# Element-wise work moved from VectorE to GpSimd, and fewer weight tiles converted ahead of the first MoE product

## The chip, the cores and the metric

One Trainium2 chip, one of its cores. The metric is device microseconds (us) of one execution; lower is better. The engines are TensorE (PE, matrix products), VectorE (DVE), ScalarE (ACT), GpSimd (POOL) and SyncE (SP, which issues the transfers). Each engine takes its instructions in the order in which the program issues them.

## The reference

Inputs are float32, the sizes 4 batches, 8 heads, 768 positions, head dimension 48. Three stages follow one another:

```python
state = 0                                    # per batch and head, 48 x 48
for t in range(768):                         # a linear attention with decay
    cur = outer(u * k[t], v[t])
    y[t] = r[t] @ (state + cur)
    state = w[t][:, None] * state + outer(k[t], v[t])
x = y as 3072 tokens x 384
x = (silu(x @ w_gate) * (x @ w_val)) @ w_out          # MoE 1, 384 -> 1536 -> 384
h = x @ w_in                                          # MoE 2, 384 -> 2048 -> 384
out = (h - tanh(h)) @ w_out2
```

## The kernel before, in words

**Attention.** The sequence is cut into chunks of 128 positions, and 24 units of work (4 chunk-and-head groups each, `NU = 24`) are walked two at a time. For each unit VectorE forms the running product of the decays with a scan (`scan`, L201), ScalarE its reciprocal by logarithm and exponential (`lnexp`), and VectorE the scaled keys `kt` (`ekx`, `ktq`) and the queries `q = r * P` (L258). TensorE multiplies `kt` by `q` (`sc`, L290), VectorE writes the upper triangle of the result over a tile `A` (`mask`, L296) whose diagonal ScalarE has filled (`fill`, L241) with the sums of r * u * k (`diag`: two products, L226 and L230, and a reduction, L233). The state is carried from chunk to chunk (`tr`, `kv`, `state`, `spread`), and `y` adds both parts (L350, L357). `out` splits y into a high and a low part for the products that follow; the rows of the last heads are put in place by six small transfers (`place`, L390), so that the tokens' tile `x` of a block of 512 tokens is complete only when these have landed.

**Order by hand.** The schedule is manual. `gap(n)` holds the attention's work as steps, nine for two units (113 in all), each a set of chains that `weave` interleaves instruction by instruction, so that the issue order is the program's. The first 25 steps run on their own; then one step goes ahead of each of the MoE's steps. A block of 512 tokens has 18 MoE steps in the first pass (6 hidden tiles, three steps each: a gate product, a value product, an output product of an earlier tile), nine matmuls of 128x128 by 128x512 each. Four units make a block; there are 6 blocks. The second pass over the MoE's other half and MoE 2 come after and have no attention in them.

**Weights.** The weights arrive as 64-bit floating-point numbers in tiles `f` of 128x384 (L71). `converter.step` puts the bits of a float32 together on VectorE (L93, L95, L97), ScalarE casts that to the high part (L77), and VectorE subtracts to get the low part (`low`, L82); cast and low part are issued in the next tile's step. Two tiles beyond the one in conversion have their load issued, with three buffers. The first 18 tiles (`c1`) serve the first blocks; 12 of them are converted ahead of the first MoE product, two before the first attention step and ten in the odd steps from 5 to 23, and then one in every second MoE step. The other tiles (`cb`) follow from the second block on, one in four steps, and go to memory.

All loads and stores are issued by SP, in the program's order, so that one that waits for its buffer or its data holds up those behind it. GpSimd only prepares constants at the start.

Of the kernel before, what the change touches and what calls it, by code (L numbers as in the profile page):

```python
# [8 lines left out]
FP32 = mybir.dt.float32  # L9
# [5 lines left out]
ALU = mybir.AluOpType  # L15
# [14 lines left out]
UB = NU // NB  # L30
# [19 lines left out]
def weave(chains):  # L50

    live = [c for c in chains if c is not None]
    while live:
        live = [c for c in live if next(c, live) is not live]


def once(fn):
    fn()
    yield


class converter:


    def __init__(self, nc, f64, stage):
        self.nc, self.f64, self.stage = nc, f64, stage
        self.loaded, self.sub = [], None

    def load(self, src):
        st = self.f64.tile([128, 384], I64, tag="f64", name="f64")  # L70
# [8 lines left out]
    def low(self):  # L79
        if self.sub:  # L80
            w, wt = self.sub
            self.nc.vector.tensor_tensor(wt[:, 1, :], w, wt[:, 0, :].bitcast(FP32), ALU.subtract)  # L82
            self.sub = None

    def step(self, wt, guard=False):
# [28 lines left out]
class attention:  # L114
# [105 lines left out]
        self.nc.scalar.activation(  # L220
            out=w, in_=w, func=AF.Relu, bias=self.wmx, accum_out=self.accw[:, u:u + 1])

    def diag(self, u):
        nc, s = self.nc, self.u[u]
        r, k = s["rk"][:, 0, :], s["rk"][:, 1, :]
        nc.vector.tensor_tensor(r, r, k, ALU.mult)  # L226
        yield
        r4 = r.rearrange("p (a c e) -> p a c e", a=2, c=2)
        ub = self.u_sb[:, u % 2, :].rearrange("p (a e) -> p a e", a=2)
        nc.vector.tensor_tensor(r4, r4, ub[:, :, None, :].to_broadcast([128, 2, 2, 96]), ALU.mult)  # L230
        yield
        s["c"] = self.odd.tile([128, 8], FP32, tag="c", name="c")
        nc.vector.tensor_reduce(s["c"], r.rearrange("p (c d) -> p c d", d=D), AX.X, ALU.add)  # L233
        yield
# [13 lines left out]
        nc.vector.tensor_tensor(s["x0"], self.k(u), s["x0"], ALU.mult)  # L248
        yield

    def ktq(self, u):
        nc, s = self.nc, self.u[u]
        s["kt"] = self.wk.tile([128, 4, 128], FP32, tag="kt", name="kt", bufs=1)
        nc.vector.scalar_tensor_tensor(
            s["kt"], s["e"], 2.0, s["x0"], ALU.subtract, ALU.mult, reverse0=True)
        yield
        s["q"] = self.wk.tile([128, 4, 128], FP32, tag="q", name="q")
        nc.vector.tensor_tensor(s["q"], self.r(u), s["P"][:, :, 0:128], ALU.mult)  # L258
        yield

    def chunks(self, u):

# [132 lines left out]
    def gap(self, n, xt, xtile):  # L395

        gi, n = divmod(n, 9)
        u0, u1, n0, n1 = range(2 * gi, 2 * gi + 4)  # L400
        up = u0 - 1
        here, ahead, behind = u0 < NU, n0 < NU, gi > 0
        x = lambda u: xt[u // UB]
        c = []
        if n == 0:
            if behind:
                c.append(self.state(up))
            if here:
                self.sc(u0)
                self.load_v(u1)  # L410
            if ahead:
                c.append(self.scan(n0))
        elif n == 1:
            if behind:
                self.spread(up)
            if here:
                c.append(self.mask(u0))
            if ahead:
                c.append(self.scan(n1))
                self.load_rk(n0)  # L420
        elif n == 2:
            if here:
                self.tr(u0)
            if behind:
                self.y(up)
            if here:
                c.append(self.ekx(u1))
            if ahead:
                self.lnexp((n0, n1))
        elif n == 3:  # L430
            if here:
                self.trc(u0)
                c.append(self.ktq(u1))
            if behind:
                c.append(self.out(up, x(up)))
            if here:
                c.append(once(lambda: self.fill(u1)))
            self.load_w(u0 + 4)
            self.load_v(n0)
        elif n == 4:  # L440
            if behind:
                self.place(up, x(up))
            if here:
                self.kv(u0)
                self.sc(u1)
            if ahead:
                c.append(self.diag(n0))
        elif n == 5:
            c += [self.state(u0), self.mask(u1)]
            if ahead:  # L450
                c.append(once(lambda: self.w_check(n0)))
            self.load_rk(n1)
            self.load_tok(u0 + 4)
        elif n == 6:
            self.spread(u0)
            self.tr(u1)
            if ahead:
                c.append(self.diag(n1))
                c.append(once(lambda: self.w_check(n1)))
        elif n == 7:  # L460
            self.trc(u1)
            self.y(u0)
            if ahead:
                c.append(self.ekx(n0))
            self.load_w(u0 + 5)
            self.load_tok(u0 + 5)
        else:
            if u0 % UB == 0:
                xt[u0 // UB] = xtile()
            self.kv(u1)  # L470
            c.append(self.out(u0, x(u0)))
            if ahead:
                c.append(self.ktq(n0))
                c.append(once(lambda: self.fill(n0)))
        return c

# [2 lines left out]
def body(ctx: ExitStack, tc: tile.TileContext, rkw, tok, vtok, ub, w1, w2, rf, kf, vf, wf, uf, out):  # L479
    nc = tc.nc  # L480
# [30 lines left out]
    conv = converter(nc, f64, stage)  # L511
# [149 lines left out]
    with tc.manual_schedule():  # L661

        pa = ExitStack()
        att = attention(nc, pa, tc, const, (rkw, tok, vtok, ub), accw, accx)
        pp_ = pa.enter_context(tc.tile_pool(name="pp", bufs=1))

        c1 = convs(seq(0), w1, wpa, W)
# [20 lines left out]
        nc.vector.memset(zsw_t, -ZSW)  # L688

        xt, ptin = {}, {}  # L690
        weave([att.scan(0)])
        weave([att.scan(1)])
        att.lnexp((0, 1))
        c1.step()
        nc.vector.tensor_copy(out=att.cm, in_=att.cmf)
        weave([att.diag(0), att.ekx(0)])
        weave([att.ktq(0), att.diag(1), c1.chain(), once(lambda: att.fill(0))])
        att.w_check(0)
        att.w_check(1)
        att.load_tok(2)  # L700
# [4 lines left out]
        def agap():  # L705
            if at[0] == steps:
                return []
            at[0] += 1
            return att.gap(at[0] - 1, xt, xtile)

        for n in range(9 * UB // 2 + 7):
            weave(agap() + ([c1.chain()] if n % 2 and n > 4 else []))

        tail = None
        for b in range(NB):
            last = b == NB - 1
            if last:
                cb.until(3 * HF)
                pa.close()
                ex = ctx.enter_context(tc.tile_pool(name="ex", bufs=3, space=PSUM))  # L720
                wpb = ctx.enter_context(tc.tile_pool(name="wpb", bufs=3 * HF))
                pb = ExitStack()
                pin = pb.enter_context(tc.tile_pool(name="pin", bufs=2))
                x2p = pb.enter_context(tc.tile_pool(name="x2p", bufs=1))
                for i in cb.order:
                    fetch(wpb, i, W)

            def gap(f, i, b=b, last=last):
                j = 3 * f + i
                chains = [] if last else agap()  # L730
                if b == 0:
                    if j % 2:
                        chains.append(c1.chain())
                    if c1.n <= j:
                        c1.until(j)
                elif b == 1 and j == 0:
                    c1.until(3 * HF)
                    cb.loads(2)
                elif j % 4 == 2:
                    chains.append(cb.chain())  # L740
                return chains

            def done(a, b=b):
                if b == NB - 1:
                    t = pin.tile([128, KD, TB], FP32, tag="pin", name="pin")
                elif b == NB - 2:
                    t = x2p.tile([128, 2, KD, TB], FP32R, tag="x2", name="x2")[:, 0].bitcast(FP32)
                else:
                    t = pp_.tile([128, KD, TB], FP32, tag="pt", name="pt")

                def copy(k):
                    nc.scalar.copy(out=t[:, k], in_=a[k])
                    if k == KD - 1:
                        if b == NB - 1:
                            ptin[b] = t
                        else:
                            nc.sync.dma_start(out=pt_d[b], in_=t)

                for k in range(KD):
                    later(k // 2, lambda k=k: copy(k))  # L760

            if b + 1 < NB:
                nc.sync.dma_start(out=xs_d[b], in_=xt[b].bitcast(FP32))
            tail = mlp(xt[b], range(HF), tail, gap, done)
# [136 lines left out]
        for j, b in enumerate(order):  # L901
            for m in range(NM):
# [14 lines left out]
                if m == 3 and j + 1 < NB:  # L917
                    n = order[j + 1]
# [26 lines left out]
        with tc.If(flag1 < 384):  # L945
# [3 lines left out]
            with ExitStack() as fb:  # L949
                fw = fb.enter_context(tc.tile_pool(name="fw", bufs=3))  # L950
                with tc.For_i(0, NB, 1) as b:
# [3 lines left out]
                    for f in range(NF):  # L955
                        wt = [fw.tile([128, 2, 384], FP32R, tag=f"fw{i}", name="fw", bufs=1) for i in range(3)]
# [7 lines left out]
                        s, t = stile("s", bufs=1), stile("t")  # L964
# [16 lines left out]
        with tc.If(flag2 < 512):  # L981
# [3 lines left out]
            with tc.For_i(0, NB, 1) as b:  # L985
# [3 lines left out]
                for m in range(NM):  # L989
                    wt = [fw.tile([128, 2, 384], FP32R, tag=f"fw{i}", name="fw") for i in range(2)]  # L990
# [161 lines left out]
```

## Time and profile before

| | |
|---|---|
| median of 3 runs | 1013.29 us (1012.47 to 1013.78) |
| profiled execution | 1014.84 us, span 1013.1 us |
| TensorE, VectorE, ScalarE, GpSimd busy | 958.1, 643.6, 508.6, 3.8 us |
| mean granted clock of TensorE | 0.974 of full speed |

A row of the profile names the engine, the source line (L82 is line 82), the operation and the tiles, output first. Busy times are sums over instructions, means are nanoseconds of one. VectorE's consecutive instructions overlap at their ends, so the distance from start to start is shorter than an instruction's duration. The span is what the profiler sees; the execution's time is some 1.7 us more.

### The profile page before, as it was taken

The page shows a single profiled execution, that of the slowest core. Times are in us where ns is not written, and L with a number is a line of the kernel's source. Part 1 is how long each engine was busy: PE and PEld are TensorE (multiplying, and loading weights), DVE is VectorE, ACT ScalarE, POOL GpSimd, SP SyncE. Part 2 cuts the span into 40 slices and gives each one's busy share as a digit, 9 for nine tenths or more (in the row PEclk, how much of TensorE's full clock was granted, in tenths as well). Part 3 has the DMA queues.
Part 4 walks back from the last instruction along what each step waited for, and adds up shares of the span by engine and source line. Part 5 has one row for each costly group of instructions (what it writes and reads, how often), then busy time and mean ns, then how long its engine had stood idle before and what let it go on. Part 6 is the DMA issues. An engine that isn't in the chain of part 4 may idle for free.

```text
span 1013.1 us, 13589 instructions
## 1 busy us (share of the span) xinstructions
PE 958.1 (95%) x5002; PEld 785.2 (77%) x5002; DVE 643.6 (64%) x1166; ACT 508.6 (50%) x1110; POOL 3.8 (0%) x16
## 2 busy tenths in 40 slices
PE   2679999999999999999999999999999999999994
PEld 2557778888888788888888887888888888888883
DVE  8999878888875424656646635666556665565442
ACT  6668777676764313323323325555455554545541
POOL 1000000000000000000000000000000000000000
PEclk9659999999999999999999999999999999999997
DMA  8567365766643481454557764344353343520001
GB/s 300 168 228 259 113 239 182 257 203 229 217 148 128 159 348 47 164 178 159 200 176 260 259 226 156 94 144 137 97 195 98 111 170 98 197 64 0 32 1 38
DMA packets 53506, 164.09 MB, mean 162 GB/s; under 512 B 6704, under 2 KB 9136, under 8 KB 50608
## 3 DMA queue, kind: packets, MB, share of 16 engines
q1 hardware_dynamic: 53424, 163.06, 47.0%
q8 instruction: 43, 0.70, 0.3%
q14 instruction: 39, 0.32, 0.1%
HBM read 122.14 MB, written 38.54 MB: 159 GB/s over the span
## 4 chain that ended last, share of the span: by engine, by line
PE 85%; DVE 9%; ACT 2%; DMA 1%; issue 1%; SPq 0%; DVEq 0%; ACTq 0%
PE p_ps L523 46%; PE a L872 19%; PE a L651 14%; PE sc_ps L290 2%; PE y_ps L357 2%; DMA f<-in_w_dram 1%; PE y_ps L350 1%; PE kv_ps L307 1%; DVE A L296 1%; DVE cvt L95 1%; DVE P L201 1%; DVE w L82 1%; DVE cvt L97 1%; DVE rk L230 1%; PE kT_ps L270 0%
## 5 line engine op out<-in xcount | busy, mean ns | idle before, releaser
L523 PE MATMUL p_ps<-x,w 128*128 128x512 f32 x2160 | 526.5, 392 | 0.0
L523 PEld LDWEIGHTS p_ps<-x,w 128*128 128x128 f32 x2160 | 402.4, 188 | 88.7 <-issue 3.9
L872 PE MATMUL a<-hi,w 128*128 128x512 f32 x576 | 192.9, 389 | 0.0
L851 DVE TENSOR_TENSOR t<-p_ps,z 128x512 f32<-128x512 f32 x96 | 66.4, 692 | 157.9 <-ACT z L849 157.9
L651 PE MATMUL a<-hi,w 128*128 128x512 f32 x432 | 146.8, 394 | 0.0
L626 DVE TENSOR_TENSOR t<-s,p_ps 128x512 f32<-128x512 f32 x72 | 49.4, 686 | 142.0 <-PE p_ps L523 133.6
L872 PEld LDWEIGHTS a<-hi,w 128*128 128x128 f32 x576 | 108.1, 188 | 22.4
L872 PE MATMUL a<-lo,w 128*128 128x512 f32 x288 | 112.4, 390 | 2.7 <-DVE lo L860 2.7
L849 ACT ACTIVATE z<-p_ps 128x512 f32<-128x512 f32 x96 | 57.5, 599 | 109.6 <-PE p_ps L523 109.5
L854 ACT CAST hi<-g 128x512 fp32r<-128x512 f32 x96 | 59.7, 622 | 77.5 <-DVE g L852 77.5
L617 ACT ACTIVATE s<-p_ps 128x512 f32<-128x512 f32 x72 | 42.9, 596 | 107.8 <-PE p_ps L523 107.7
L651 PEld LDWEIGHTS a<-hi,w 128*128 128x128 f32 x432 | 81.1, 188 | 17.5
L630 ACT CAST hi<-t 128x512 fp32r<-128x512 f32 x72 | 44.7, 621 | 94.8 <-DVE t L626 94.2
L651 PE MATMUL a<-lo,w 128*128 128x512 f32 x216 | 84.3, 390 | 0.0
L852 DVE SCALAR_TENSOR_TENSOR g<-zs,t 128x512 f32<-128x512 f32 x96 | 66.5, 693 | 10.3 <-ACT zs L850 0.5
L850 ACT ACTIVATE zs<-z,sa_t 128x512 f32<-128x512 f32 x96 | 69.7, 726 | 3.1
L872 PEld LDWEIGHTS a<-lo,w 128*128 128x128 f32 x288 | 54.0, 188 | 15.0 <-DVE lo L860 3.9
L860 DVE TENSOR_TENSOR lo<-g,hi 128x512 fp32r<-128x512 f32 x96 | 65.6, 683 | 0.1
L634 DVE TENSOR_TENSOR lo<-t,hi 128x512 fp32r<-128x512 f32 x72 | 49.6, 689 | 19.3 <-ACT hi L630 19.3
L290 PE MATMUL sc_ps<-q,kt 64*128 64x128 f32 x384 | 36.1, 323 | 26.5 <-DVE q L258 25.2
L241 ACT ACTIVATE A<-ident,c 128x128 f32<-128x128 f32 x192 | 58.9, 400 | 2.5 <-DVE c L233 2.5
L290 PEld LDWEIGHTS sc_ps<-q,kt 64*128 64x128 f32 x384 | 30.3, 221 | 31.7 <-DVE q L258 16.2
(86 smaller groups left out, 822.3 us busy)
## 6 DMA issues: line engine op xcount, KB each, us to landing
f<-in_w_dram SPq DMA_DIRECT2D x68, 384.0 KB, 4.0
ck<-in_w_dram SPq DMA_DIRECT2D x68, 384.0 KB, 3.1
rkd<-in_rkw_dram SPq DMA_DIRECT2D x24, 512.0 KB, 4.8
w_d<-ws SPq DMA_DIRECT2D x32, 384.0 KB, 2.6
w<-w_d SPq DMA_DIRECT2D x32, 384.0 KB, 7.2
rk<-in_tok_dram SPq DMA_DIRECT2D x24, 384.0 KB, 5.7
x_d<-x SPq DMA_DIRECT2D x6, 1536.0 KB, 6.1
x<-x_d SPq DMA_DIRECT2D x6, 1536.0 KB, 6.9
```

Source lines behind the costliest of these rows:

```text
L241: self.nc.scalar.activation(out=a[:, h, i, :], in_=self.ident, func=AF.Copy, scale=s["c"][:, 2 * i + h:2 * i + h + 1])
L290: self.nc.tensor.matmul(s["sc"][h][:, i * 128:(i + 1) * 128], s["kt"][hs, i, :], s["q"][hs, i, :])
L523: nc.tensor.matmul(ps, wt[:, part, k * 128:(k + 1) * 128], x[:, xp_, k, :], start=(n == 0), stop=(n == 3 * KD - 1))
L634: nc.vector.tensor_tensor(h["l"], h["t"], h["h"].bitcast(FP32), ALU.subtract)
L651: nc.tensor.matmul(acc[0][k], a, c, start=(first and i == 0), stop=(last and i == 2))
L849: nc.scalar.activation(out=z, in_=ps, func=AF.Square, accum_out=accz[:, i:i + 1])
L850: nc.scalar.activation(out=s, in_=z, func=AF.Square, scale=C2 ** 0.5, bias=sa_t)
L851: nc.vector.tensor_tensor(hz, ps, z, ALU.mult)
L852: nc.vector.scalar_tensor_tensor(g, s, C2 * SB, hz, ALU.add, ALU.mult)
L854: nc.scalar.copy(out=gh, in_=g)
L860: nc.vector.tensor_tensor(gl, g, gh.bitcast(FP32), ALU.subtract)
L872: nc.tensor.matmul(a[k], c, g, start=(m == 0 and n == 0), stop=(m == NM - 1 and n == 2))
```

## The change

Four things are done at once.

- The two diagonal products and the query product are issued to GpSimd instead of VectorE (`diagm`, `qx`), earlier in the nine steps than they stood: query products in steps 1 and 6 instead of 3 and 8, diagonal products in steps 2 and 4 instead of 4 and 6. The diagonal's reduction stays on VectorE in its step (`diagr`). The query tile has three buffers instead of two.
- The low parts of the first 18 weight tiles are computed by GpSimd; from the second block on, `low` is VectorE's again.
- Ahead of the first MoE product 6 tiles are converted instead of 12: two before the steps and four in steps 20 to 23. In the first block then one tile in every MoE step instead of every second one.
- 24 attention steps instead of 25 run ahead of the first MoE step.

```diff
@@ converter
+        self.low_engine = nc.vector
...
-            self.nc.vector.tensor_tensor(wt[:, 1, :], w, wt[:, 0, :].bitcast(FP32), ALU.subtract)
+            self.low_engine.tensor_tensor(wt[:, 1, :], w, wt[:, 0, :].bitcast(FP32), ALU.subtract)
@@ attention
-    def diag(self, u):
+    def diagm(self, u):
         nc, s = self.nc, self.u[u]
         r, k = s["rk"][:, 0, :], s["rk"][:, 1, :]
-        nc.vector.tensor_tensor(r, r, k, ALU.mult)
-        yield
+        nc.gpsimd.tensor_tensor(r, r, k, ALU.mult)
         r4 = r.rearrange("p (a c e) -> p a c e", a=2, c=2)
         ub = self.u_sb[:, u % 2, :].rearrange("p (a e) -> p a e", a=2)
-        nc.vector.tensor_tensor(r4, r4, ub[:, :, None, :].to_broadcast([128, 2, 2, 96]), ALU.mult)
-        yield
+        nc.gpsimd.tensor_tensor(r4, r4, ub[:, :, None, :].to_broadcast([128, 2, 2, 96]), ALU.mult)
+
+    def diagr(self, u):
+        nc, s = self.nc, self.u[u]
+        r = s["rk"][:, 0, :]
         s["c"] = self.odd.tile([128, 8], FP32, tag="c", name="c")
         nc.vector.tensor_reduce(s["c"], r.rearrange("p (c d) -> p c d", d=D), AX.X, ALU.add)
         yield
-    def ktq(self, u):
+    def ktx(self, u):
...
-        s["q"] = self.wk.tile([128, 4, 128], FP32, tag="q", name="q")
-        nc.vector.tensor_tensor(s["q"], self.r(u), s["P"][:, :, 0:128], ALU.mult)
-        yield
+
+    def qx(self, u):
+        nc, s = self.nc, self.u[u]
+        s["q"] = self.wk.tile([128, 4, 128], FP32, tag="q", name="q", bufs=3)
+        nc.gpsimd.tensor_tensor(s["q"], self.r(u), s["P"][:, :, 0:128], ALU.mult)
@@ gap: n == 1
                 c.append(self.mask(u0))
+                self.qx(u1)
@@ gap: n == 2
                 self.lnexp((n0, n1))
+                self.diagm(n0)
@@ gap: n == 3
-                c.append(self.ktq(u1))
+                c.append(self.ktx(u1))
@@ gap: n == 4
-                c.append(self.diag(n0))
+                c.append(self.diagr(n0))
+                self.diagm(n1)
@@ gap: n == 6
-                c.append(self.diag(n1))
+                c.append(self.diagr(n1))
+                self.qx(n0)
@@ gap: n == 8
-                c.append(self.ktq(n0))
+                c.append(self.ktx(n0))
@@ body
+        conv.low_engine = nc.gpsimd
...
-        weave([att.diag(0), att.ekx(0)])
-        weave([att.ktq(0), att.diag(1), c1.chain(), once(lambda: att.fill(0))])
+        att.qx(0)
+        att.diagm(0)
+        att.diagm(1)
+        weave([att.ekx(0), att.diagr(0)])
+        weave([att.ktx(0), att.diagr(1), c1.chain(), once(lambda: att.fill(0))])
...
-        for n in range(9 * UB // 2 + 7):
-            weave(agap() + ([c1.chain()] if n % 2 and n > 4 else []))
+        lead = 9 * UB // 2 + 6
+        for n in range(lead):
+            weave(agap() + ([c1.chain()] if n > lead - 5 else []))
...
                 if b == 0:
-                    if j % 2:
-                        chains.append(c1.chain())
+                    chains.append(c1.chain())
                     if c1.n <= j:
                         c1.until(j)
                 elif b == 1 and j == 0:
                     c1.until(3 * HF)
+                    conv.low_engine = nc.vector
                     cb.loads(2)
```

## Rows read from the trace of the kernel before

**Rows 1.** The page: busy tenths of TensorE in 40 slices, and the chain by engine.
```profile
PE   2679999999999999999999999999999999999994
...
PE 85%; DVE 9%; ACT 2%; DMA 1%; issue 1%; SPq 0%; DVEq 0%; ACTq 0%
```
**Rows 2.** Windows: length, then busy us (instructions) by engine, clock, DMA share, GB/s.
```profile
0.00:15.70 15.70, 2.16 (x17) 1.94 (x18) 11.58 (x29) 8.32 (x21) 3.84 (x16) 1.00 0.88 327
15.70:75.60 59.90, 38.11 (x284) 31.61 (x284) 58.44 (x119) 40.88 (x113) 0.00 (x0) 0.66 0.63 207
75.60:129.90 54.30, 53.02 (x379) 42.55 (x377) 50.03 (x98) 41.06 (x100) 0.00 (x0) 0.99 0.59 197
```
**Rows 3.** Groups by line on VectorE, 15.7 to 75.6 us: busy, mean | idle before.
```profile
L201 DVE TENSOR_TENSOR_SCAN P<-w,rst 128x516 f32<-128x516 f32 x6 | 7.3, 1223 | 0.0
L82 DVE TENSOR_TENSOR w<-cvt,w 128x384 fp32r<-128x384 f32 x11 | 6.1, 552 | 0.0
L97 DVE SCALAR_TENSOR_TENSOR cvt<-f,cvt 128x384 int32<-128x384 int32 x10 | 5.5, 555 | 0.2
L95 DVE SCALAR_TENSOR_TENSOR cvt<-f,cvt 128x384 int32<-128x384 int32 x10 | 5.5, 552 | 0.0
L93 DVE TENSOR_SCALAR cvt<-f 128x384 int32<-128x384 int32 x10 | 3.5, 350 | 0.0
...
L258 DVE TENSOR_TENSOR q<-rkd,P 128x512 f32<-128x512 f32 x5 | 3.4, 684 | 0.0
...
L230 DVE TENSOR_TENSOR rk<-rk,u_sb 128x384 f32<-128x384 f32 x6 | 3.3, 556 | 0.1
L226 DVE TENSOR_TENSOR rk<-rk 128x384 f32<-128x384 f32 x6 | 3.3, 552 | 0.0
```
**Rows 4.** Timeline of VectorE: start, duration, instruction.
```profile
43.23 0.68 DVE L258 TENSOR_TENSOR q<-rkd,P 128x512 f32<-128x512 f32 x1
43.84 0.41 DVE L377 TENSOR_TENSOR x<-y_ps,x 128x256 fp32r<-128x256 f32 x1
...
49.58 0.55 DVE L226 TENSOR_TENSOR rk<-rk 128x384 f32<-128x384 f32 x1
50.04 0.35 DVE L93 TENSOR_SCALAR cvt<-f 128x384 int32<-128x384 int32 x1
50.31 0.55 DVE L230 TENSOR_TENSOR rk<-rk,u_sb 128x384 f32<-128x384 f32 x1
```
**Rows 5.** Groups by line on ScalarE, 15.7 to 75.6 us.
```profile
L77 ACT CAST w<-cvt 128x384 fp32r<-128x384 f32 x10 | 5.0, 504 | 0.0
L334 ACT COPY SE<-S 64x96 f32<-64x96 f32 x18 | 4.9, 270 | 14.6 <-DVE S L324 14.4
```
**Rows 6.** Timeline of GpSimd in the first 5 us.
```profile
1.92 0.64 POOL L153 TENSOR_SCALAR_AFFINE_SELECT cmf<-cmf 128x512 f32<-128x512 f32 x1
2.50 2.09 POOL L159 MEMSET SE<- 128x256 f32 x8
```
**Rows 7.** Timeline of VectorE in the first 6 us.
```profile
3.65 2.36 DVE L201 TENSOR_TENSOR_SCAN P<-w,rst 128x516 f32<-128x516 f32 x2 [1.93 <-DMA w<-in_rkw_dram]
```
**Rows 8.** Timeline of TensorE about the first MoE product, and in the third block.
```profile
71.60 2.21 PE L350 MATMUL y_ps<-q,SE 128*128 128x128 f32 x8
...
75.64 2.58 PE L523 MATMUL p_ps<-x,w 128*128 128x512 f32 x9
...
232.03 4.40 PE L523 MATMUL p_ps<-x,w 128*128 128x512 f32 x18
```
**Rows 9.** Timeline of SyncE's queue: issues of the placing transfers and of the store behind.
```profile
68.22 3.78 SPq L390 DMA_DIRECT2D x<-yo  x6
...
232.64 3.78 SPq L390 DMA_DIRECT2D x<-yo  x6
...
237.90 0.34 SPq L763 DMA_DIRECT2D xs_d<-x  x1
```
**Rows 10.** Issues of the first 130 us: count, KB each, median us from issue to landing.
```profile
f<-in_w_dram SPq DMA_DIRECT2D x20, 384.0 KB, 5.7
```

## The prediction

> **What bounds the kernel now.** I read the chain that ended last first. TensorE holds 85% of it and VectorE 9% [rows 1], so the whole is a TensorE kernel; VectorE can matter only where TensorE has holes. The busy row by slices shows where these are: 2, 6 and 7 tenths in the first three of 40 slices, then 9 nearly to the end [rows 1]. Next I cut the start into stages by the busy times of the engines [rows 2]. Up to 15.7 us the data arrive. From 15.7 to 75.6 us, 59.9 us in which 25 steps of the attention are walked ahead of the first MoE product (it starts at 75.64 us [rows 8]), VectorE is busy 58.4 us, ScalarE 40.9 and TensorE 38.1 at a granted clock of 0.66. VectorE is the bound there. From 75.6 to 129.9 us, the first block of 18 MoE steps, TensorE is busy 53.0 of 54.3 us and VectorE 50.0: TensorE sets the pace, VectorE is close behind. So what VectorE sheds before 75.6 us moves all that follows; in the first block it has only some 4 us to spare, and later relief of VectorE is worth nothing, since TensorE is full.
>
> **What the change takes off VectorE ahead of the first product.** VectorE's instructions overlap at their ends, so I cost them from start to start: 0.46 us for a 128x384 product (49.58 to 50.04), 0.27 for the tensor-scalar of a conversion (50.04 to 50.31), 0.61 for a 128x512 product (43.23 to 43.84) [rows 4]. In this stage stand 11 low parts (L82), 10 conversions (L93, L95, L97), 5 query products (L258) and 6 pairs of diagonal products (L226, L230) [rows 3].
> - Low parts to GpSimd: 11 x 0.46 = 5.1 us.
> - Ten conversions become four: 6 x (0.27 + 2 x 0.46) = 7.1 us.
> - Diagonal products: 12 x 0.46 = 5.5 us.
> - Query products: 5 x 0.61 = 3.1 us.
> - The 25th step (one reduction of VectorE, some 0.5 us) goes behind the first product.
>
> Sum 21.3 us; VectorE keeps 37.1. The others don't shrink as much: ScalarE loses six casts of 0.50 us [rows 5] and keeps about 37, TensorE keeps 38.1 if its clock stays. So the stage cannot shrink by 21: three engines end up equal, each waiting on the others. ScalarE's 14.4 us of waiting for VectorE's state [rows 5] is the hand-over that shortens as VectorE clears. The next stage shows two engines at 98% and 92% of the time at once [rows 2], so the software pipeline is deep enough for high shares.
>
> **What GpSimd's instructions cost.** It gets, in this stage, 12 diagonal products, 5 query products and 4 low parts. The trace has no two-input instruction on GpSimd. The nearest row is the 128x512 affine select with one input, 0.64 us [rows 6]; scaled to 384 columns it is 0.48. One pass over the data is the lower bound, two passes (0.96 and 1.28) the upper, since a product reads two tensors where the select reads one. I take 0.85 and 1.1 us, nearer the upper: 16 x 0.85 + 5 x 1.1 = 19 us of some 47. GpSimd has room. The Trainium skill (GPSIMD Engine Reference, Elementwise) gives 4497 ns for a 2048-column product on GpSimd; an estimate by that page is 0.84 and 1.12 us, and no run here shows it yet.
>
> **What GpSimd's work costs VectorE.** The two engines may get in each other's way. The only row where both work side by side is a pair of VectorE scans with two SBUF inputs, 2.36 us for two from 3.65 us on [rows 7], beside GpSimd's memsets from 2.50 to 4.59 us [rows 6]: 1.18 each, against a mean of 1.22 later [rows 3]. So no price, but the memset only writes. Lower bound zero; upper bound all of GpSimd's time, 19 us here. Nearer the one row that there is, I take a quarter, 5 us: VectorE 42 us, and at the 92% share of the next stage a stage of 46; I take 47. **Term 1: 59.9 - 47 = 12.9 us gained.** Ends: 37.1 / 0.92 = 40 without a price (20 us gained), 56 / 0.975 = 57.5 at the full one (2.4 gained). Ahead of the stage, the diagonal products leave the head of VectorE's queue, but its reductions wait for GpSimd's: **term 2: 1 us gained** (0 to 2).
>
> **The first block.** Conversions go from 6 to 12, +7.1 us on VectorE; 7 low parts go (-3.2), 4 pairs of diagonal products (-3.7) and 4 query products (-2.4). VectorE's load falls from 50.0 to about 48, but it sits in the first 12 steps. GpSimd gets 12 low parts, 8 diagonal and 4 query products, about 21 us; a quarter of that on VectorE is 5. With 53 of 54.3 us there is little to absorb it. **Term 3: 3 us lost** (0 to 15).
>
> The weights' loads are pulled along: one per step instead of one per two. They stand in SP's queue behind the six small placing transfers (L390), whose issue alone takes 3.8 us [rows 9] and which wait for VectorE's last output parts; a load needs a median of 5.7 us to land [rows 10]. With three buffers a load is issued two steps, some 6 us, ahead of its use, where it was 12. Behind a placing, 3.8 + 5.7 exceeds 6 by 3.5 us, and VectorE's in-order queue stands behind the conversion that waits: masks and the MoE's products too. It happens once in the block and once just ahead of it. **Term 4: 2 us lost** (0 to 7).
>
> **Lead one step shorter.** Each block's first product now comes one step sooner after the placing. Fourth block: the step with the placing starts its nine products at 232.03 us; 18 take 4.4 [rows 8]. Today a third group and another attention product stand between; then only those 4.4 us do, so the product would start near 236.5. The last placing is issued at 236.4 and x is complete by 237.90 (the store that waits for it goes out then) [rows 9]. The product wants the slice that comes last only at its third matmul, 0.5 us in: a wait of 0.9. VectorE's shorter queue brings the placing forward by about the 0.6 us of the query product. **Term 5: five blocks at 0.5, 2.5 us lost** (0 to 6). At the first block the shorter lead cuts the 4.0 us of a y product at half clock (71.60 to 75.64 [rows 8]); the placing ended issue at 72.0 [rows 9] and lands 1.5 later, and the y product runs behind it instead: no net.
>
> The query's third buffer and GpSimd's queue I cost at nothing: the query product is issued three steps, some 6 us, ahead of its use, which covers its 1.1. Without that cover each score product would wait up to 1.1 us.
>
> **Sum.** -12.9 - 1 + 3 + 2 + 2.5 = -6.4 us. The span of 1013.1 becomes 1006.7, the profiled execution's own 1014.84 becomes 1008.4, and the median of 1013.29 becomes 1006.9: **1007 us**, its own range 1001 to 1011.
>
> **Rivals.**
> - GpSimd and VectorE exclude each other. It is the place of terms 1 and 3: a product of GpSimd that reads SBUF holds up each VectorE instruction with two SBUF inputs. For it: scans, conversions, e, x0 and kt products all have two such inputs, and GpSimd's instruction is longer than the one that it replaces. Against it: masks, reductions, states and outputs do not, and VectorE would have holes in the shorter stage. At the full price, -2.4 - 1 + 15 + 2 + 2.5 = +16, 1029 us. At half, the stage is (37.1 + 9.5) / 0.92 = 51 (9 gained) and the block loses about 7: +1.5, 1015. From about 45% of GpSimd's time on it decides; at 70%, midway of the two, **1021 us**. Chance 25%. The Trainium skill (SBUF — State Buffer, Who interferes with whom) states just this: such a pair contends, and whichever starts first holds the shared port for its whole instruction. The row with the scans does not contradict it, as the page exempts a GpSimd instruction that only writes; no run here shows it yet.
> - Everything packs: no price on VectorE, loads in time, 40 us for the stage: -20 - 1 + 2.5 = -18.5, **995 us**. Three engines near full and TensorE's clock at 0.66 speak against it; more TensorE work per time could raise that clock. Chance 13%.
> - The gain is given back: the stage ends at 50 us (-10), the block pays 5, loads 3.5 and placings 5 less the front's 1: +2.5, within a few us of **1013 us**. Chance 15%.
>
> The forecast keeps 47%. What a measurement of this kernel can tell from no change is 0.2%, 2 us. Faster: forecast 47 + packed 12 = 59%; same 14%; slower 27% (the exclusion and a little of the third). The range 995 to 1021 holds about 8 in 10; what lies beyond is mainly the full price of exclusion.
>
> **What would show it.** First product near 62 us instead of 75.64; VectorE below 92% up to there; VectorE's two-input instructions at today's durations, 0.55, 0.68 and 1.22 us (longer ones, on lines the change did not touch, mean exclusion); a first block of 57 to 60 us; VectorE waiting for a weight load once or twice; TensorE waiting under 1 us for the placing at each block's start. A first product before 62 but a block over 65 us would make the prediction wrong, as would a stage still bound by VectorE.

## The result, and the profile after

The changed kernel takes 1020.8 us (median of 4, 1019.3 to 1021.8) against 1013.45 (4 runs, 1012.5 to 1013.8): a ratio of 1.0075, 95% interval 1.006 to 1.009. It is slower by three quarters of a per cent, where 0.6% faster was forecast. The profiled execution's span is 1019.9 us.

The page after, parts 2 and 4 (GpSimd's busy tenths, and the chain by engine), where [rows 1] stood before:

```profile
POOL 7354622222230000000000000000000000000000
...
PE 87%; DVE 7%; DMA 2%; issue 1%; ACT 1%; SPq 0%; POOL 0%; DVEq 0%; ACTq 0%; POOLq 0%
```

TensorE still sets the whole, so the loss must again be holes at the start. Windows after, cut at the first MoE product (69.28 us) and at the first of the second block (138.50); columns as in [rows 2]:

```profile
0.00:14.00 14.00, 0.00 (x0) 0.00 (x0) 6.89 (x18) 5.14 (x11) 8.37 (x21) 1.00 0.86 311
14.00:69.28 55.28, 33.83 (x276) 28.65 (x277) 49.69 (x72) 39.78 (x112) 29.16 (x22) 0.80 0.53 175
69.28:138.50 69.22, 60.06 (x379) 47.97 (x378) 62.73 (x100) 42.96 (x105) 32.41 (x27) 0.89 0.57 186
```

The first product is 6.4 us sooner (75.64 before), but the first block takes 69.2 us where it took 54.3. Behind it 1.8 us come back (881.4 against 883.2 us to the end). VectorE, with 47 instructions fewer in the stage ahead of the product, is still busy 49.7 us there, and 62.7 in the block, where about 48 were forecast. So its instructions have become longer. VectorE's groups by line from 14.0 to 69.3 us, to be held against [rows 3] (L202 is the scan, L94 to L98 the conversion, L257 the keys, L329 and L326 the state, L301 the mask, L236 the reduction):

```profile
L202 DVE TENSOR_TENSOR_SCAN P<-w,rst 128x516 f32<-128x516 f32 x6 | 10.0, 1666 | 0.0
L301 DVE COPY_PREDICATED A<-cm,sc_ps 128x512 f32<-128x512 uint32 x11 | 7.9, 719 | 3.0 <-PE sc_ps L295 3.0
L257 DVE SCALAR_TENSOR_TENSOR kt<-e,x 128x512 f32<-128x512 f32 x6 | 5.6, 935 | 0.5
...
L96 DVE SCALAR_TENSOR_TENSOR cvt<-f,cvt 128x384 int32<-128x384 int32 x4 | 3.7, 936 | 0.1
...
L236 DVE TENSOR_REDUCE c<-rk 128x8 f32<-128x384 f32 x6 | 3.3, 543 | 0.0
L94 DVE TENSOR_SCALAR cvt<-f 128x384 int32<-128x384 int32 x4 | 3.2, 806 | 0.0
L329 DVE TENSOR_TENSOR S<-S,P 128x96 f32<-128x96 f32 x6 | 3.2, 533 | 0.1
L326 DVE TENSOR_TENSOR S<-S,kv_ps 128x96 f32<-128x96 f32 x7 | 1.7, 240 | 0.0
```

The lengthening sorts by operands, not by size or place. Two inputs in SBUF: the scan 1.67 us (1.22 before), a conversion's second step 0.94 (0.55), the state times P 0.53 (0.25). The tensor-scalar with one input: 0.81 (0.35). An input in PSUM, or a single one in a reduction: the mask 0.72, the state plus kv 0.24, the reduction 0.54, all as before (0.72, 0.25 and 0.55). None of these instructions was touched by the change. How it happens is seen instruction by instruction. The timelines of GpSimd and of VectorE between 52 and 57 us:

```profile
52.39 1.18 POOL L264 TENSOR_TENSOR q<-rkd,P 128x512 f32<-128x512 f32 x1 [11.16 <-DMA rkd<-in_rkw_dram]
53.53 1.92 POOL L227 TENSOR_TENSOR rk<-rk 128x384 f32<-128x384 f32 x1
55.53 0.99 POOL L230 TENSOR_TENSOR rk<-rk,u_sb 128x384 f32<-128x384 f32 x1
```

```profile
52.70 1.97 DVE L202 TENSOR_TENSOR_SCAN P<-w,rst 128x516 f32<-128x516 f32 x1
54.59 0.98 DVE L329 TENSOR_TENSOR S<-S,P 128x96 f32<-128x96 f32 x1
55.60 0.26 DVE L326 TENSOR_TENSOR S<-S,kv_ps 128x96 f32<-128x96 f32 x1
```

GpSimd's query product runs undisturbed, 1.18 us. The scan that VectorE issues 0.3 us into it is 0.75 us too long. The diagonal product that GpSimd issues during the scan is 0.93 us too long in its turn, and the state's product behind, 0.25 us of work, waits for that one's end. The next state instruction has an input in PSUM and runs beside GpSimd's next product in 0.26, near its mean of 0.24.

Over all lines the excess over the means of the kernel before is 12.1 us in the first stage (scan 6 x 0.44, keys 6 x 0.25, e and x0 1.5, conversions 4.7, state 6 x 0.28; some 2.6 of it between 14.0 and 19.1 us, ahead of the steps) and 14.2 in the block, 26.3 us for 49 instructions of GpSimd: 0.54 us each, where VectorE had spent 0.46 or 0.61 on the same work.

### The profile page after: what moved, and what is told of

Same layout as the page of the kernel before. It is cut to its first block, busy times and chain, and to the rows that moved or that the text cites. A ratio compares the mean times of both kernels' runs of the same rounds, so it can differ in the third digit from the quotient of the medians.

```text
span 1019.9 us, 13712 instructions
## 1 busy us (share of the span) xinstructions
PE 960.0 (94%) x5002; PEld 787.2 (77%) x5002; DVE 641.9 (63%) x1076; ACT 509.5 (50%) x1110; POOL 119.1 (12%) x106
## 4 chain that ended last, share of the span: by engine, by line
PE 87%; DVE 7%; DMA 2%; issue 1%; ACT 1%; SPq 0%; POOL 0%; DVEq 0%; ACTq 0%; POOLq 0%
PE p_ps L532 47%; PE a L886 19%; PE a L660 14%; PE sc_ps L295 2%; PE y_ps L362 2%; PE y_ps L355 2%; DMA f<-in_w_dram 1%; DVE P L202 1%; PE kv_ps L312 1%; DVE cvt L96 1%; PE kT_ps L275 1%; DVE A L301 1%; DMA rkd<-in_rkw_dram 1%; DVE cvt L94 1%; DVE cvt L98 0%
## 5 line engine op out<-in xcount | busy, mean ns | idle before, releaser
L863 ACT ACTIVATE z<-p_ps 128x512 f32<-128x512 f32 x96 | 57.5, 599 | 109.7 <-PE p_ps L532 109.6
L643 DVE TENSOR_TENSOR lo<-t,hi 128x512 fp32r<-128x512 f32 x72 | 52.9, 735 | 25.7 <-ACT hi L639 25.7
```

The source lines that it names most:

```text
L643: nc.vector.tensor_tensor(h["l"], h["t"], h["h"].bitcast(FP32), ALU.subtract)
L863: nc.scalar.activation(out=z, in_=ps, func=AF.Square, accum_out=accz[:, i:i + 1])
```

## The experiments

A is the theory that GpSimd's products hold up VectorE; B is that the new order of the weights costs. The first four runs were made to tell them apart. A ratio is a run's time over that of the kernel before, with its 95% interval.

**The order alone.** The kernel before with the change's last two hunks only:

```diff
-        for n in range(9 * UB // 2 + 7):
-            weave(agap() + ([c1.chain()] if n % 2 and n > 4 else []))
+        lead = 9 * UB // 2 + 6
+        for n in range(lead):
+            weave(agap() + ([c1.chain()] if n > lead - 5 else []))
...
-                    if j % 2:
-                        chains.append(c1.chain())
+                    chains.append(c1.chain())
```

> The new order of the weights and the shorter lead alone, every product back on VectorE. Theory A (exclusion: a product of GpSimd holds up VectorE's instructions with two SBUF inputs): VectorE sheds 7.1 us of conversions ahead of the first product, which comes near 68 us instead of 75.6; the first block has 7.1 us of conversions and 5 more low parts (2.3 us) on a VectorE that was 92% busy, so it takes about 62 us instead of 54; the sum is near no change, 1013 us (1010 to 1017). Theory B (the order of the weights is what costs: loads that come late behind the placing transfers and 12 conversions in 12 steps): the first block takes some 69 us as in the changed kernel, and the time is 1020 us or more.

1.0019 (1.0008 to 1.003). The windows, cut at the first product of the first and of the second block:

```profile
15.00:62.01 47.01, 27.54 (x260) 23.10 (x261) 44.73 (x86) 36.76 (x102) 0.00 (x0) 0.86 0.60 197
62.01:129.37 67.36, 56.76 (x379) 45.29 (x378) 60.06 (x124) 43.15 (x105) 0.00 (x0) 0.90 0.60 199
```

Both theories are half right. The time is A's, 0.2% above the kernel before; but the block is long, 67.4 us, as B had it, and the first product comes at 62.0, sooner than A had it. VectorE's conversions are moved from one stretch to the next, not hidden: VectorE is the busiest engine in both (44.7 of 47.0 us, 60.1 of 67.4). In this trace the second block begins at 129.4 us, against 129.95 in the kernel before, so where the 0.19% lie is not shown.

**The engines alone.** The changed kernel with the old order of the weights and a lead of 25 (the two hunks undone).

> The moves to GpSimd alone, with the kernel before's order of the weights (12 tiles ahead, one in two steps) and its lead of 25 steps. Theory A: ahead of the first product VectorE sheds 13.7 us of products, but 28 instructions of GpSimd hold it up by some 0.55 us each, 15 us: first product at 75 to 78 us; the first block has less on VectorE (50.0 - 9.3 + 19 x 0.55 = 51 us) and takes 54 to 57 us; 1013 to 1020 us. Theory B: VectorE is relieved for nothing, first product near 65 us, block 54 us, 1003 us.

1.0054 (1.0037 to 1.0071): A, and more of it ahead of the first product than A said:

```profile
82.99 3.33 PE L532 MATMUL p_ps<-x,w 128*128 128x512 f32 x9
```

The product comes 7.3 us later than in the kernel before, though VectorE lost 13.7 us of work; the block takes 54.4 us, as before. 0.19% and 0.54% make 0.73%, within the noise of the change's 0.75%.

**GpSimd busy, but reading nothing.**

```diff
-        nc.gpsimd.tensor_tensor(r, r, k, ALU.mult)
...
+        for _ in range(4):
+            nc.gpsimd.memset(r, 0.0)
...
-        nc.gpsimd.tensor_tensor(s["q"], self.r(u), s["P"][:, :, 0:128], ALU.mult)
+        for _ in range(2):
+            nc.gpsimd.memset(s["q"], 0.0)
```

and likewise two memsets for a low part.

> The changed kernel with each of GpSimd's products replaced by memsets of the same output for about the same time (two for a low part, four for a pair of diagonal products, two for a query product), so that GpSimd is as busy but reads nothing; the low parts of the first 18 tiles, the diagonal and the queries are then zeros. Theory A: VectorE's two-input instructions are back at 0.55, 0.69 and 1.22 us, the first product comes near 60 us, the block takes 56 to 60 us, 1003 us (998 to 1009). Theory B (order of the weights, or the longer way over GpSimd's queue): 1018 us or more, the block near 69.

0.9953 (0.9939 to 0.9968), 1008.6 us: 12 us less than the changed kernel, though GpSimd is busy 22.9 and 18.3 us in the two stretches and the order is the same. (It is busy 29.2 and 32.4 us in the changed kernel, and a memset also waits for fewer inputs, so the 12 us are not the reading alone.) The windows, cut at the second matmul of the first product (59.69 us) and at the first product of the second block, and VectorE's groups, 14 to 75 us:

```profile
14.00:59.69 45.69, 28.98 (x266) 23.92 (x264) 37.86 (x73) 37.71 (x107) 22.91 (x53) 0.88 0.62 210
59.69:123.67 63.98, 57.45 (x376) 46.03 (x377) 48.40 (x97) 42.71 (x104) 18.27 (x42) 0.90 0.63 211
...
L206 DVE TENSOR_TENSOR_SCAN P<-w,rst 128x516 f32<-128x516 f32 x6 | 7.3, 1222 | 0.0
L100 DVE SCALAR_TENSOR_TENSOR cvt<-f,cvt 128x384 int32<-128x384 int32 x8 | 4.4, 550 | 0.1
L259 DVE SCALAR_TENSOR_TENSOR kt<-e,x 128x512 f32<-128x512 f32 x6 | 4.1, 689 | 0.4
```

All are back at their old means; only the one-input tensor-scalar (0.41 us between 14 and 140 us, 0.35 before) is not quite. The first product begins at 58.7 us; between its first and its third matmul it waits 0.7 us for the placing transfers. From 59.7 us the block takes 64.0, longer than A said, though VectorE has only 48.4 us to do in it: it waits 9.4 us there for weights (11.4 between 14 and 140 us).

**The price by itself.** A kernel of its own, 16 VectorE instructions of a form (8 scans), with nothing, products or memsets on GpSimd beside them.

> Not the reference's computation at all: 16 VectorE instructions of one form after another, alone and beside GpSimd products of 128x384 or beside GpSimd memsets. Theory A: beside products, VectorE's 0.46 us of a 128x384 two-input product rises towards 1 us or more, the scan of 512 towards 2 us, and GpSimd's product of 0.99 us is stretched too; instructions with an input in PSUM, masked copies and reductions keep 0.6, 0.6 and 0.46 us; beside memsets the two-input product keeps 0.46. The tensor-scalar with one input, 0.27 us, is slowed as in the changed kernel. Theory B: all keep their lone intervals.

Its timeline (first and main rows of the phases): VectorE's two-input products alone, beside 12 products of GpSimd, and beside memsets; the tensor-scalar beside 8 products and beside memsets; products of VectorE with an input in PSUM beside 10 of GpSimd; and 12 products of GpSimd alone.

```profile
5.30 9.44 DVE L90 TENSOR_TENSOR o<-a,b 128x384 f32<-128x384 f32 x16
...
14.78 17.53 DVE L90 TENSOR_TENSOR o<-a,b 128x384 f32<-128x384 f32 x16
...
15.43 15.29 POOL L82 TENSOR_TENSOR p<-d,e 128x384 f32<-128x384 f32 x12
...
32.35 9.46 DVE L94 TENSOR_TENSOR o<-a,b 128x384 f32<-128x384 f32 x16
...
57.01 14.55 DVE L102 TENSOR_SCALAR t<-w 128x384 int32<-128x384 int32 x16
...
71.60 7.72 DVE L106 TENSOR_SCALAR t<-w 128x384 int32<-128x384 int32 x16
...
79.31 11.51 DVE L110 TENSOR_TENSOR o<-a,ps 128x512 f32<-128x512 f32 x16
...
79.61 10.69 POOL L82 TENSOR_TENSOR p<-d,e 128x384 f32<-128x384 f32 x10
...
114.24 12.77 POOL L82 TENSOR_TENSOR p<-d,e 128x384 f32<-128x384 f32 x12
```

Twelve products cost VectorE 17.53 - 9.44 = 8.1 us, 0.67 each, and are themselves stretched from 1.06 to 1.27 us; memsets cost nothing (9.46). With an input in PSUM VectorE takes 0.72 from start to start, masked copies 0.76, reductions 0.58, more than the 0.6, 0.6 and 0.46 expected. They were not run alone; but the durations (0.69, 0.73 and 0.55) are those of the kernel before, and GpSimd's products beside them keep 1.07 to 1.08. The tensor-scalar takes 14.6 us for 16 beside 8 products and 7.7 beside 8 memsets; its durations, 0.88 and 0.45 us, are both above the 0.35 of the kernel before. The Trainium skill (SBUF — State Buffer, Who interferes with whom) has these forms right: two SBUF inputs contend with a GpSimd instruction that reads, one input in PSUM does not, a writing one does not disturb a two-input instruction. The lock for the whole instruction that the same page states (section SBUF: two separate sides) would make the second phase 9.4 + 12.8 = 22.2 us if it covered all the time from start to start; it took 17.5, so by this estimate 4.7 of GpSimd's 12.8 us ran beside VectorE.

**The loads' place.** The loads of the 18 tiles issued by ScalarE from the first step to the end of the first block (`self.queue.dma_start` for `self.nc.sync.dma_start`), in the changed kernel, with the order alone, and with the memsets.

> The changed kernel with the loads of the first 18 weight tiles issued by ScalarE instead of SyncE from the first attention step to the end of the first block, so that none stands behind a placing transfer. If the loads' place in SyncE's queue costs (term 4): VectorE's 6.8 us of waiting for weights ahead of the second block falls under 2, and the time to 1016 to 1018 us. If only exclusion and the sum of VectorE's work count: the waits may go, the time stays at 1019 to 1021 us. A third way: ScalarE's own order delays the loads or its casts, and the time rises above 1022.

> The new order of the weights alone, all products on VectorE, with the loads issued by ScalarE as in the run before. If the loads' place costs, VectorE's 3.8 us of waiting in the first block goes and the time falls from 1015.8 to some 1012 to 1013 us; if it does not, 1015 to 1016.

> As the run with memsets for GpSimd's products (low parts, diagonal and queries of the first stages are zeros), and the weights' loads issued by ScalarE. There VectorE had 48.4 us of work in a block of 64 us and waited 11.4 us for weights ahead of the second block. If the loads' place in SyncE's queue is what holds it (term 4): the waits fall under 4 us, the block to 57 to 60 us, the time from 1008.6 to 1002 to 1005 us. If it is the transfers themselves: no change.

1.0083 (1.0066 to 1.01), 0.9998 (0.9989 to 1.0008) and 0.9927 (0.991 to 0.9944). In the changed kernel the waits for weights between 14 and 140 us fall from 3.4 to 1.4 us and nothing is gained (the 6.8 us of the expectation count 3.0 at 146.6 us, in the second block). With the order alone and with the memsets 0.2 to 0.3% are gained. With the memsets the trace shows it: the second block begins at 121.5 us, 2.1 sooner. With the order alone it begins at 129.3 us as without (129.4), so there the place of the gain is not shown. With the memsets 7.9 of 11.4 us of waiting remain, 5.4 of them between 60 and 78 us, where the DMA engines are busy 0.92 to 1.00 of the time. So the place in the queue is a smaller part of the waiting; whether the rest is the transfers themselves or the three buffers that a load must wait for, no run separates.

**One kind at a time**, all with the new order: low parts; the query (twice: first with the diagonal products on VectorE at the change's places, then in the old places); the diagonal products.

> The new order of the weights, and of the three kinds of products only the low parts of the first 18 tiles on GpSimd. Exclusion: VectorE sheds 17 x 0.46 = 7.8 us and is held up by 17 x 0.55 = 9.4 us, so 1016 to 1019 us, against 1015.8 without. If a low part on GpSimd were free: 1008 to 1010 us. If GpSimd's late low parts make the products wait: above 1020.

> The new order of the weights, and of the three kinds only the query product on GpSimd (diagonal products on VectorE, in the steps of the changed kernel). Exclusion: ten products in the first 130 us shed 6.1 us and hold VectorE up by 10 x 0.6 to 0.8: no difference to 1015.8, 1014 to 1018 us. If free: 1009 to 1011 us.

> The new order of the weights, all else as in the kernel before but for the query product, which alone goes to GpSimd at its new place (the diagonal products stay in VectorE's chains, which the last run with the query alone had moved too). Exclusion alone: ten products shed 6.1 us of VectorE ahead of the second block and hold it up by 0.6 to 0.9 each, so 1014 to 1018 us, beside 1015.8 without; the first product near 60 to 62 us. If the run before lost its 5.6 us ahead of the first product to the query on GpSimd and not to the diagonal's new place: first product near 67, 1017 us.

> The new order of the weights, and of the three kinds only the diagonal products on GpSimd, at the places of the changed kernel. By difference (changed kernel 1020.8; order alone 1015.8; low parts +1.2; query -2.9) they cost 6.7 us: 1022 us (1021 to 1024) if the three add up. If they cost no more than exclusion by 20 products in the first 130 us (20 x 0.55 - 20 x 0.46 = 2 us): 1017 to 1019, and the rest is what the three do to one another in GpSimd's queue.

Low parts 1.0034 (1.0021 to 1.0047), as A had it. Query 1.0038 (1.0024 to 1.0052), but with the diagonal products in their old chains 0.9994 (0.9982 to 1.0006), below the order alone: the first query run lost by the diagonal products' new place, on VectorE too. That the query on GpSimd pays a little is not shown: the interval only just clears that of the order alone, and in its trace the second block begins at 130.5 us, 1.1 later than with the order alone. Diagonal products 1.0127 (1.011 to 1.0144), more than the whole change: the three kinds do not add.

**Ahead of the steps.** The timeline of VectorE in the changed kernel:

```profile
12.53 0.55 DVE L236 TENSOR_REDUCE c<-rk 128x8 f32<-128x384 f32 x1 [3.64 <-POOL rk L230]
...
19.12 2.02 DVE L202 TENSOR_TENSOR_SCAN P<-w,rst 128x516 f32<-128x516 f32 x1
```

The first reduction waits 3.64 us for GpSimd's products, and the steps' first scan starts at 19.12 us (15.73 before).

```diff
-        att.diagm(0)
-        att.diagm(1)
-        weave([att.ekx(0), att.diagr(0)])
-        weave([att.ktx(0), att.diagr(1), c1.chain(), once(lambda: att.fill(0))])
+        weave([att.diag(0), att.ekx(0)])
+        weave([att.ktx(0), att.diag(1), c1.chain(), once(lambda: att.fill(0))])
```

> The changed kernel with the diagonal products of the first two units only back on VectorE, in the order of the kernel before (before the attention steps). In the changed kernel VectorE's first reduction waits 3.6 us for GpSimd's products and the steps begin at 19.1 us instead of 15.7. If that delay lasts to the end (term 2 had the wrong sign): 1017 to 1018 us instead of 1020.8. If VectorE makes it up in the steps, where it is held up by exclusion all the same: 1020 to 1021.

> As the run before, with the first two units' diagonal products back on VectorE as in the first run of the three. If the late begin is what the diagonal products cost: 3 to 4 us below the run before. If their stalls in the steps are: within 1.5 us of it.

1.0045 (1.0031 to 1.0059), 1019.0 us, between the two forecasts: 0.3% of the 0.75% is this place. With the diagonal products alone on GpSimd it gives back the same 0.3% (1.0095, 1.0077 to 1.0113), again between the forecasts, and the intervals touch. That what remains of them are their stalls within the steps is argued, not shown.

**What did not cost, together.**

> The two parts that did not cost, together: the new order of the weights with the query product alone on GpSimd (1012.9 us by itself) and the weights' loads issued by ScalarE (1013.0 by itself; 2.8 us less than without). If both add: 1010 us (1008 to 1012), faster than either kernel; if they relieve the same wait of VectorE: 1012 to 1014.

> As the run before, but with 25 attention steps ahead of the first MoE step instead of 24. If the shorter lead made the products wait for the placing transfers (term 5): 1 to 3 us faster than the run before; the changed kernel's trace shows no such wait, so otherwise no difference beyond 1.5 us.

0.9999 (0.999 to 1.0008) and 1.0007 (0.9998 to 1.0016): no gain over the kernel before, and no effect of the lead. Of the versions that leave nothing out, none is faster than the kernel before by more than the measurement tells.

## Why the prediction was wrong

Cut at the first scan of the steps (15.73 us before, 19.12 after) and at the first products of the two blocks, forecast and traces compare so:

| stretch | forecast | measured |
|---|---|---|
| ahead of the steps (term 2) | 1 us gained | 3.4 lost |
| steps to the first product (term 1) | 12.9 gained | 9.7 gained (59.9 to 50.2) |
| first block (terms 3 and 4) | 5 lost | 14.9 lost (54.3 to 69.2) |
| behind it (term 5) | 2.5 lost | 1.8 gained |
| sum | 6.4 gained | 6.8 lost |

- **What bounds.** Right: the loss arises ahead of the second block, and TensorE keeps its pace behind it.
- **What VectorE sheds.** Right as a count: 37.1 us were to remain ahead of the first product; with GpSimd not reading, 37.9 were busy. In the block 48 were forecast and 48.4 found.
- **GpSimd's own cost.** 0.85 and 1.1 us were taken, 0.99 and 1.18 are the undisturbed durations in the changed kernel, nearer still to two passes. The estimate by the Trainium skill's page, 0.84 and 1.12, was short by a similar amount; the page's figure is for an addition.
- **The first step that failed is the price on VectorE** ("Nearer the one row that there is, I take a quarter"). The row, scans beside memsets, showed a GpSimd that only writes, and the text said so; the two also overlap for only 0.9 of the scans' 2.36 us. Its zero said nothing of products. Taken were 5 us in each stretch; 12.1 and 14.2 were paid, 66% of the 40 us that I had estimated for GpSimd's time. With the old order of the weights (the engines alone), 13.7 us of shed work end in a first product 7.3 us later, the new places of the products included.
- **The second step that failed is what VectorE's relief brings without any price**: 40 us for the stage at a share of 92%, and a block that loses nothing by VectorE because its load falls to about 48 us. The sum holds 7 + 3 us for the price, so without it it would be 997 us. The run with memsets, where VectorE has the forecast work and its old durations, takes 1008.6, more than the forecast with the price in it. Its first product begins at 58.7 us where 40 us for the stage would give about 55, and 9.7 of the block's 14.9 us are lost there too. In that block VectorE waits 9.4 us for weights (term 4 has 2), and TensorE is busy 57.5 us at a clock of 0.90, not 53.0 at 0.99; what each of the two costs, no run separates. The order alone says the same: 62.0 us to the first product, 67.4 for the block, +0.19%, so moving conversions into the block, entered as 7.1 us gained, is worth nothing.
- **The rival of exclusion** was priced at 70% and 1021 us, with a chance of 25%, and its cause came true. That its time came out too is in part luck: its scale runs from 997 us without a price to 1029 at the full one, where 1008.6 was measured without and 1020.8 at 66%.
- **Term 2 had the wrong sign.** The text saw that the reductions would wait for GpSimd's products and did not add up the queue: query, two products and so on at 1 us each after the loads land, against 0.46 on VectorE. The longer VectorE instructions add some 2.6 us there.
- **Term 4** (loads, 2 us lost): moving the loads to another queue gave 2.6 us with the memsets and nothing in the changed kernel, where VectorE waits only 3.4 us for weights. So the queue's place was about right in size, and the waiting for weights as a whole was not.
- **Term 5** (the shorter lead, 2.5 us lost) did not occur: TensorE never waits for a placing transfer in the changed kernel, and 25 steps instead of 24 gave no gain. Where the first product comes sooner, with the memsets, it waits 0.7 us for one.
- **A slip without effect.** ScalarE's remainder is 40.9 - 6 x 0.50 = 37.9 us, not 37.
- **Open.** Why the diagonal products alone on GpSimd cost 1.27% while all three kinds together cost 0.75%. The trace of the first shows the block at 72.8 us with TensorE's clock at 0.87, but no run separates the clock's part.

## What to carry to other kernels

Before giving GpSimd element-wise work to relieve VectorE, sort VectorE's instructions by operands: here those with two SBUF inputs, and the one-input tensor-scalar, paid 0.54 us for a GpSimd product (0.67 in a dense stream), about what the product took on VectorE (0.46 or 0.61); those with an input in PSUM and reductions kept their durations. A row in which two engines merely work side by side is no price unless both use the operands in question. Work moved along an engine that bounds both stretches has not gone anywhere. And relief of one engine is worth only what the next limit leaves: test it with the work left out before pricing what stands against it. Here that was 0.47%, some 5 us, with VectorE down by 21 us ahead of the first product.

## What the runs showed that I had not expected

A hole in TensorE's work costs more than its length. Windows of the changed kernel in the first block, and matmuls of TensorE there:

```profile
78.00:84.00 6.00, 1.29 (x14) 0.79 (x13) 3.94 (x8) 3.14 (x10) 0.99 (x1) 0.79 1.00 404
84.00:90.00 6.00, 6.00 (x27) 5.00 (x28) 5.93 (x10) 2.23 (x6) 2.81 (x3) 0.64 0.66 210
90.00:96.00 6.00, 6.00 (x45) 5.03 (x44) 5.96 (x8) 4.59 (x10) 4.31 (x3) 1.00 0.22 66
```

```profile
69.28 4.19 PE L532 MATMUL p_ps<-x,w 128*128 128x512 f32 x9
...
85.83 5.55 PE L532 MATMUL p_ps<-x,w 128*128 128x512 f32 x18
...
120.33 4.38 PE L532 MATMUL p_ps<-x,w 128*128 128x512 f32 x18
```

From 78 to 84 us TensorE is busy 1.3 of 6 us, while the DMA engines are full (1.00, 404 GB/s) and VectorE waits 2.0 us for a weight tile. In the next 6 us the granted clock is 0.64, a mixture of 2.4 and 1.2 GHz, and 18 matmuls take 5.55 us, where 18 of the same form at full clock take 4.38. For its 379 matmuls TensorE is busy 60.1 us in this block and 53.0 in [rows 2], so 7 of the block's 14.9 us are matmuls made slower rather than matmuls waiting. Not all of them come from holes in the block: the first product, behind a stage in which TensorE is busy 33.8 of 55.3 us, takes 4.19 us for its nine matmuls (2.58 in [rows 8]). The other blocks with the new order that were cut in this way have TensorE busy 56.8 us (order alone, clock 0.90) to 62.5 (diagonal products alone on GpSimd, the first two units' back on VectorE, clock 0.83).
